# V loaded four keys a partition and put in order by 0/1 products, with experts and slot inputs turned round, in an attention and soft-MoE kernel

## The chip, the cores and the metric

One core of one Trainium2 chip runs the whole kernel. The metric is the time of one execution in device microseconds; the time before is the median of three runs. The profile is one further execution, taken by the hardware profiler, with its own time.

## The reference

Attention over 16 beacon keys and 576 causal keys, for 8 batches of 8 heads, and behind it a soft mixture of experts over all 4608 tokens:

```python
B, H, S, Nb, D = (8, 8, 576, 16, 64)
k_all = np.concatenate([beacon_k, k], axis=2)
v_all = np.concatenate([beacon_v, v], axis=2)
scores = scale * np.matmul(q, k_all.transpose(0, 1, 3, 2))
scores = np.where(causal, -1000000000.0, scores)
a = softmax(scores)                      # over the 592 keys
x = (a @ v_all).transpose(0, 2, 1, 3).reshape(B * S, H * D)   # 4608 x 512
logits = x @ phi                         # 32 slots
d = softmax(logits, over tokens); c = softmax(logits, over slots)
slot_input = d.T @ x                     # 32 x 512, 4 slots for each of 8 experts
slot_out[e] = relu(slot_input[e] @ w1[e]) @ w2[e]             # w1 512 x 1024, w2 1024 x 512
out = c @ slot_out
```

(The softmaxes are written out in the reference, with the maximum subtracted.) Inputs and output are float32.

## The kernel before

Attention works through 32 pairs of heads, four pairs to a batch. The 592 keys and queries of a head are cut into five chunks, four of 128 and one of 80. Each engine runs its own queue strictly in the order in which the kernel records it; there is no scheduler. That order is a hand-written list of words for each pair (`order`, `lists`), the same for pairs with the same number modulo four, and `do` turns a word into instructions:

- `S0` to `S3` (`score`, L280): the score products of a pair into one of two PSUM tiles `scs`, one exp on ScalarE into `ex`, and the causal masks on GpSimd (`mask`, L278). S1 and S3 use the one tile, S0 and S2 the other, and `S0` belongs to the next pair. A list ends, for instance, in `S3 c1 T S0`.
- `A0`, `A1` (`attend`): the products of exp and V for the two heads of the *previous* pair, 15 products a head with a column of ones for the sum. Behind A1, VectorE divides into `xb` (L323, L324).
- `T` (`transp`, L266): 36 small transposes that turn q and k of the pair after the next into `qT`, `kT`, through two `tr` tiles in PSUM that VectorE empties (L268).
- `X01`, `X23`, `X4`, `L0`, `L1`, `D`, `SI`: the routing of an earlier batch: x transposed, logits, their exps `dT` transposed (L405), and the slot inputs (`si_piece`, L416).
- `c0`, `c1`, `cl`: V cast to float16 on GpSimd, from the tiles `vr` and `vl` into `vh`. `d0`, `d1` (`dup`, L335) and `M` (`mask_f`, L306) are on VectorE.

All of T, X, L, D and SI draw their PSUM tiles in turn from one pool, `ps_tr`, with two buffers; a new tile waits until the last reader of the tile before the last is done.

V comes with two neighbouring keys in a partition, 512 bytes in one run (`load_r`), so chunk 0 holds the even keys of the first 256 and chunk 1 the odd ones, and the scores pick their keys with a step of two. The diagonal blocks are folded: 64 rows of each of the two halves make one block (`f_`), whose products take `vd`, a copy of V with the halves apart, 130 columns wide. The beacon's V rows overwrite the first 8 partitions of the first tile (`load_bv`), and that request waits on SP for the tile's own load.

All loads of q, k and V are issued from SP, the 37 loads of expert weights from GpSimd at the ends of the pairs by a table (`want`). A q or k tile has five buffers.

Behind the last pair come the last batch's logits and slot inputs, then the experts: `layer1` with the weights stationary and the slot inputs moving (32 products of 32 columns an expert), a ReLU, and `layer2` with the weights moving, 512 columns in four column groups. `idle_work` is products whose result nobody reads. At last each token's output is one product and one scaling.

The pool of the two tiles and the lists:

```python
ps_tr = ctx.enter_context(tc.tile_pool(name="ps_tr", bufs=2, space=PSUM))
order = ["d1 S1 A0 L1 M S2 A1 S3 cl T S0 D", "S1 A0 X01 M S2 SI A1 S3 T S0",
         "S1 A0 X23 X4 M S2 A1 S3 c0 T S0", "d0 S1 A0 L0 M S2 A1 S3 c1 T S0"]
```

Of the kernel before, what the change touches and what calls it, by code (L numbers as in the profile page):

```python
# [8 lines left out]
FP = mybir.dt.float32  # L9
# [8 lines left out]
def kernel(  # L18
# [12 lines left out]
    nc = tc.nc  # L31
# [22 lines left out]

    def f_(s):
        return [(64 * r, 64, 2 * P * r + s, 2, 2 * P * r, P, P * s) for r in range(2)]

    steps = [  # L60
        f_(0) + f_(1) + [(0, P, 2 * P, 2, 3 * P, U - 3 * P, 2 * P)],
        [(0, P, 2 * P + 1, 2, 3 * P, U - 3 * P, 0), (0, UL, 4 * P, 1, 4 * P, UL, 208)],
        [(0, P, 0, 2, P, U - P, 0)],
        [(0, P, 1, 2, P, U - P, 0)],
# [4 lines left out]
    XF, XG1, XT, XG0 = (0, P), (2 * P, 464), 672, (752, 1216)  # L69

    POS = [0, 2, 1, 3, 4]
    prods = [(P, XF[0], P, 0, 0, 2)] + [(P, XG0[s] + P, P, s, 1, 1) for s in range(2)]
    prods += [(P, XF[1], P, 1, 0, 2)]
    prods += [(P, XG0[s], P, s, 2, 1) for s in range(2)]
    prods += [(P, XG0[s] + 2 * P, P, s, 3, 1) for s in range(2)]
    prods += [(P, XG1[s], P, 2 + s, 3, 1) for s in range(2)]  # L80
    prods += [(P, XG0[s] + 3 * P, UL, s, 4, 1) for s in range(2)]
    prods += [(P, XG1[s] + P, UL, 2 + s, 4, 1) for s in range(2)] + [(UL, XT, UL, 4, 4, 1)]
    first, final = {0, 4, 6, 10}, {3, 5, 9, 14}
# [31 lines left out]
    vrows = v.rearrange("b h s d -> (b h s) d")  # L115

    def load_r(b, r):
        t = vrp.tile([P, H, 2 * D], FP, name="vr", tag="vr")
        vr[(b, r)] = t
        o = b * H * S + 2 * P * r - Nb  # L120
        if b == 0 and r == 0:
            nc.sync.dma_start(
                out=t[:, 1:H, :], in_=vrows[S - Nb:S - Nb + (H - 1) * S].rearrange(
                    "(h s) d -> h s d", s=S)[:, 0:2 * P, :].rearrange(
                        "h (p t) d -> p h (t d)", t=2))
            nc.sync.dma_start(
                out=t[Nb // 2:P, 0, :],
                in_=v[0, 0, 0:2 * P - Nb, :].rearrange("(p t) d -> p (t d)", t=2))
        elif r == 0:
            nc.sync.dma_start(out=t[:, :, :], in_=vrows[o:o + H * S].rearrange(  # L130
                "(h s) d -> h s d", s=S)[:, 0:2 * P, :].rearrange("h (p t) d -> p h (t d)", t=2))
        else:
            nc.sync.dma_start(out=t[:, :, :], in_=v[b, :, 2 * P - Nb:4 * P - Nb, :].rearrange(
                "h (p t) d -> p h (t d)", t=2))

    def load_bv(b):
        nc.sync.dma_start(out=vr[(b, 0)][0:Nb // 2],
                          in_=beacon_v[b].rearrange("h (p t) d -> p h (t d)", t=2))
# [14 lines left out]

    def load_w(x):
        if x < NV:
            m, hs = x, (0, 1)
            t = (wh if x < NW else vrp).tile([P, 2048], F16, name="w", tag="w" if x < NW else "vr")
        else:
            m, hs = NV + (x - NV) // 2, ((x - NV) % 2,)
            t = qkp.tile([P, J * P], F16, name="wx", tag=homes[x - NV])  # L160
# [14 lines left out]
    def w1c(e, c, t):  # L175
        lo = 2 * P * (t // 2) + t % 2
        return wv[(4 * e + c // 2, c % 2)][:, lo:lo + 2 * P - 1:2]

# [7 lines left out]
    nc.sync.dma_start(out=bkf, in_=beacon_k.rearrange("b h n d -> (h n) b d"))  # L186
    load_pair(1)
    load_r(0, 0)
    load_pair(2)
    load_bv(0)  # L190
    load_r(0, 1)
    load_vl(0)
    load_pair(3)
    load_pair(4)
# [11 lines left out]
    fmask = const.tile([P, 2 * P], F16, name="fmask")  # L206
    fm = const.tile([P, 2, P], F16, name="fm")
    nc.gpsimd.memset(fm[:, :, :], 65504.0)
    for base, lo in ((P, 64), (0, 0)):
        nc.gpsimd.affine_select(out=fm[:, :, :], in_=fm[:, :, :], compare_op=AL.is_ge,  # L210
                                fill=0.0, base=base, pattern=[[-1, 2], [1, P]],
                                channel_multiplier=-2)
        nc.gpsimd.tensor_copy(out=fmask[lo:lo + 64, :].rearrange("p (s t) -> p s t", s=2),
                              in_=fm[lo:lo + 64, :, :])
# [7 lines left out]
    vd = [const.tile([P, 2, 2, H, DD], F16, name=f"vd{i}") for i in range(2)]  # L222
    for i in range(2):
        nc.vector.memset(vd[i][:, :, :, :, :], 0.0)
# [6 lines left out]
    nc.vector.memset(siacc[:, :, :], 0.0)  # L231
    siT = const.tile([P, NDC, NSL], F16, name="siT")
    hTz = const.tile([P, E, NFC, NSL], F16, name="hTz")
# [47 lines left out]
    def score(n, st):  # L281
# [3 lines left out]
        for (p0, kn, k0, ks, u0, un, col) in steps[st]:  # L285
            for a in range(2):
                nc.tensor.matmul(  # L287
                    sc[p0:p0 + kn, a, col:col + un],
                    kT[n % 3][64 * a:64 * a + 64, k0:k0 + ks * (kn - 1) + 1:ks],
                    qT[n % 3][64 * a:64 * a + 64, u0:u0 + un],  # L290
                    start=True, stop=True)
# [4 lines left out]
        if st == 0:  # L296
            mask(x[:, :, XG1[0]:XG1[0] + P], [[0, 2], [1, P]], P, -2)
        if st == 1:
            mask(x[:, :, XG1[1]:XG1[1] + P], [[0, 2], [1, P]], P - 1, -2)
            mask(x[0:UL, :, XT:XT + UL], [[0, 2], [1, UL]], 0, -1)  # L300
        if st >= 2:
            mask(x[:, :, XG0[st - 2]:XG0[st - 2] + P], [[0, 2], [1, P]], P + 2 - st, -2)

    def mask_f(n):
        x = ex[n][:, :, 0:2 * P]
        nc.vector.tensor_tensor(out=x, in0=x, in1=fmask[:, :].unsqueeze(1).broadcast_to(  # L306
            [P, 2, 2 * P]), op=AL.min)

    def attend(n, a):
        b, g = divmod(n, H // 2)  # L310
        h = 2 * g + a
        for j, (kn, o, m, c, pos, w) in enumerate(prods):
            dst = avs[0:m, a, pos * DD:(pos + w) * DD]
            if w == 2:
                dst, rhs = dst.rearrange("p (r d) -> p r d", r=2), vd[b % 2][:, c, :, h, :]
            else:
                rhs = vh[b % 2][0:kn, c, h, :]
            nc.tensor.matmul(dst, ex[n][0:kn, a, o:o + m], rhs,  # L318
                             start=j in first, stop=j in final)
# [9 lines left out]
    def cast_r(b, r, eng):  # L329
        eng.tensor_copy(  # L330
            out=vh[b % 2][:, 2 * r:2 * r + 2, :, 0:D].rearrange("p s h d -> p h s d"),
            in_=vr.pop((b, r))[:, :, :].rearrange("p h (s d) -> p h s d", s=2))

    def dup(b, r):
        nc.vector.tensor_copy(out=vd[b % 2][64 * r:64 * r + 64, :, r, :, :],  # L335
                              in_=vh[b % 2][0:64, 2 * r:2 * r + 2, :, :])
# [7 lines left out]
    def xt_piece(b, cs):  # L344
# [3 lines left out]
        for ii, i in enumerate(cs):  # L348
            m = P if i < 4 else UL
            for t in range(NDC):  # L350
                nc.tensor.transpose(  # L351
                    tp[:, ii, t, 0:m],
                    xb[b % 2][0:m, POS[i], 2 * t:2 * t + 2, :].rearrange("p h d -> p (h d)"),
                    idh[0:m, 0:m])
# [318 lines left out]
```

## Time and profile before

| what | value |
| --- | --- |
| median of three runs | 214.31 us (213.91 to 215.2) |
| the profiled execution | 212.98 us, span 211.3 us, mean granted TensorE clock 0.962 |
| TensorE, weight loads | 163.6 us busy in 3526 matmuls, 114.8 us |
| VectorE, ScalarE, GpSimd | 137.0, 127.2 and 114.0 us busy |
| exp of the scores, L294 | 107.3 us, 128 of 870 ns |
| masks on GpSimd, L278 | 62.0 us, 160 of 404 ns |
| score products, L287 | 53.1 us, 576 of them |
| attend, L318 | 44.8 us (65 columns and fewer rows), 22.8 us (130 columns) |
| V casts on GpSimd, L330 | 15.8 us, 15 of 1052 ns |
| M on VectorE, L306; doubling, L335 | 14.8 us, 32 of 464 ns; 9.0 us, 16 of 562 ns |
| weights: 27 loads of 512 KB, 10 of 256 KB | 9.5 us and 11.0 us from issue to landing |
| V: 15 loads of 512 KB | 10.7 us from issue to landing |

A line such as "62.74 0.21 PE L351 MATMUL tr<-idh,xb ... x1 [2.11 <-issue]" of a timeline gives the start and the length in microseconds, the engine, the line of the kernel, the operation, output and inputs, how many like it were merged, and, in brackets, how long the engine stood idle before and what ended that. "Issue" means that nothing which the profile records was waited for. A matmul's length contains some 0.17 us until its result stands in PSUM; the next one can start long before. L12 is line 12 of the kernel before.

### The profile page before, as it was taken

How to read it: one execution, taken by the hardware profiler on the slowest of the kernel's cores; microseconds unless marked ns; L12 is line 12 of the kernel's file. 1: busy time of each engine (PE TensorE's matmuls, PEld its weight loads, DVE VectorE, ACT ScalarE, POOL GpSimd, SP SyncE). 2: the span in 40 equal slices, each digit the busy share in tenths (PEclk: the TensorE clock that was granted, in tenths of full speed). 3: DMA queues.
4: the chain of work that ended last, by engine and by line, in shares of the span. 5: the costliest groups of instructions: out<-in, count | busy, mean ns of one | idle time of the engine just before them, and what ended most of it. 6: DMA issues, size and time to landing. Idle time of an engine off the chain costs nothing.

```text
span 211.3 us, 8131 instructions
## 1 busy us (share of the span) xinstructions
PE 163.6 (77%) x3526; PEld 114.8 (54%) x3526; DVE 137.0 (65%) x284; ACT 127.2 (60%) x185; POOL 114.0 (54%) x264
## 2 busy tenths in 40 slices
PE   2475997997859898887989998798899987888000
PEld 2333765865646676665657776565666764333000
DVE  5747595796658787866996887697856300299200
ACT  2171694897649777875986896697593111199100
POOL 5054389497647765865785897798678210000000
PEclk9999997899999999999999999999999999999755
DMA  6989999999999999999999999999999998089996
GB/s 196 283 197 339 334 284 275 270 268 273 306 254 280 301 229 284 320 278 271 292 276 255 305 266 243 269 215 210 211 212 214 207 210 166 0 298 413 413 414 250
DMA packets 44954, 55.89 MB, mean 265 GB/s; under 512 B 9087, under 2 KB 25975, under 8 KB 44919
## 3 DMA queue, kind: packets, MB, share of 16 engines
q1 hardware_dynamic: 36135, 38.60, 57.7%
q0 software_dynamic: 8784, 16.78, 42.9%
q8 instruction: 27, 0.44, 0.8%
q14 instruction: 8, 0.07, 0.1%
HBM read 62.71 MB, written 9.44 MB: 341 GB/s over the span
## 4 chain that ended last, share of the span: by engine, by line
PE 60%; issue 10%; DVE 10%; DMA 5%; POOL 4%; ACT 2%; SPq 1%; DVEq 0%; ACTq 0%; POOLq 0%
PE av L318 19%; PE sc L287 15%; PE tr L266 8%; DMA vr<-in_v_dram 5%; PE tr L595 4%; PE tr L351 3%; DVE osb L637 3%; PE tr L366 3%; DVE xb L324 2%; PE av L606 2%; ACT ex L294 2%; PE tr L416 2%; POOL ex L278 1%; PE sc L454 1%; DVE qT L268 1%
## 5 line engine op out<-in xcount | busy, mean ns | idle before, releaser
L294 ACT ACTIVATE ex<-sc 128x928 f16<-128x928 f32 (+1 forms) x128 | 107.3, 870 | 45.7 <-PE sc L287 42.3
L278 POOL TENSOR_SCALAR_AFFINE_SELECT ex<-ex 128x256 f16<-128x256 f16 (+1 forms) x160 | 62.0, 404 | 47.5 <-ACT ex L294 47.1
L287 PE MATMUL sc<-qT,kT 64*64 64x128 bf16 (+3 forms) x576 | 53.1, 272 | 4.2 <-issue 1.8
L318 PEld LDWEIGHTS <-ex 128*128 128x128 f16 (+2 forms) x960 | 41.4, 107 | 13.8 <-issue 8.4
L318 PE MATMUL av<-vh,ex 128*128 128x65 f16 (+2 forms) x832 | 44.8, 200 | 3.4 <-POOL ex L278 1.7
L287 PEld LDWEIGHTS <-kT 64*64 64x64 bf16 (+2 forms) x576 | 21.2, 105 | 18.6 <-issue 11.5
L324 DVE TENSOR_TENSOR xb<-av,r 128x640 f16<-128x640 f32 x32 | 26.4, 824 | 1.1
L268 DVE COPY qT<-tr 128x576 bf16<-128x576 bf16 x32 | 23.9, 748 | 2.1 <-PE tr L266 2.1
L268 DVE COPY kT<-tr 128x576 bf16<-128x576 bf16 x32 | 23.9, 747 | 0.8 <-PE tr L266 0.8
L318 PE MATMUL av<-vd,ex 128*128 128x130 f16 x128 | 22.8, 229 | 0.5 <-issue 0.5
L266 PE MATMUL tr<-idb,kf 64*64 64x64 bf16 x576 | 16.0, 200 | 6.2 <-DVE bkT L253 3.4
L266 PE MATMUL tr<-idb,qf 64*64 64x64 bf16 x576 | 16.6, 202 | 4.5 <-DMA qf<-in_q_dram 3.7
L169 POOL DMA_DIRECT2D w<-in_moe_w_dram x27 | 19.4, 721 | 0.0
L266 PEld LDWEIGHTS <-qf 64*64 64x64 bf16 x576 | 12.7, 115 | 11.3 <-issue 6.3
L356 DVE COPY xT<-tr 128x1024 f16<-128x1024 f16 x14 | 9.7, 691 | 13.4 <-PE tr L351 13.4
L266 PEld LDWEIGHTS <-kf 64*64 64x64 bf16 x576 | 13.1, 116 | 6.7 <-issue 6.4
L330 POOL CAST vh<-vr 128x1024 f16<-128x1024 f32 x15 | 15.8, 1052 | 0.0
L306 DVE TENSOR_TENSOR ex<-ex,fmask 128x512 f16<-128x512 f16 x32 | 14.8, 464 | 0.4
L634 ACT ACTIVATE osb<-fp,rc 128x512 f32<-128x512 f32 x18 | 11.3, 685 | 4.5 <-PE fp L632 3.8
L351 PE MATMUL tr<-idh,xb 128*128 128x128 f16 (+1 forms) x140 | 10.3, 216 | 4.0 <-issue 4.0
L637 DVE TENSOR_SCALAR osb<-fp,rc 128x512 f32<-128x512 f32 x18 | 12.3, 746 | 0.7 <-PE fp L632 0.7
L632 PE MATMUL fp<-soh,eLh 128*128 128x512 f16 x36 | 10.6, 377 | 2.4 <-ACT osb L634 1.6
(75 smaller groups left out, 148.5 us busy)
## 6 DMA issues: line engine op xcount, KB each, us to landing
w<-in_moe_w_dram POOLq DMA_DIRECT2D x27, 512.0 KB, 9.5
qf<-in_q_dram SPq DMA_DIRECT2D x32, 288.0 KB, 7.4
kf<-in_k_dram SPq DMA_DIRECT2D x32, 288.0 KB, 8.1
out_dram<-osb SPq DMA_DIRECT2D x16, 512.0 KB, 5.5
vr<-in_v_dram SPq DMA_DIRECT2D x15, 512.0 KB, 10.7
wx<-in_moe_w_dram POOLq DMA_DIRECT2D x10, 256.0 KB, 11.0
vl<-in_v_dram SPq DMA_DIRECT2D x8, 160.0 KB, 6.3
out_dram<-osb SPq DMA_DIRECT2D x4, 256.0 KB, 2.9
```

Source lines behind the costliest of these rows:

```text
L169: nc.gpsimd.dma_start(out=t[:, 0:1024 * len(hs)].rearrange("p (c f) -> p c f", f=1024), in_=src)
L266: nc.tensor.transpose(tp[po:po + 64, j, :], hi, idb[po:po + 64, po:po + 64])
L268: nc.vector.tensor_copy(out=dst[:, Nb:Nb + S].rearrange("p (s j) -> p s j", j=J), in_=tp[:, :, :].rearrange("p j s -> p s j"))
L278: nc.gpsimd.affine_select(out=x, in_=x, compare_op=AL.is_ge, fill=0.0, base=base, pattern=pattern, channel_multiplier=cm)
L287: nc.tensor.matmul(sc[p0:p0 + kn, a, col:col + un], kT[n % 3][64 * a:64 * a + 64, k0:k0 + ks * (kn - 1) + 1:ks], qT[n % 3][64 * a:64 * a + ...
L294: nc.scalar.activation(x[:, :, o:o + w], sc[:, :, 0:w], AF.Exp, scale=scale)
L306: nc.vector.tensor_tensor(out=x, in0=x, in1=fmask[:, :].unsqueeze(1).broadcast_to([P, 2, 2 * P]), op=AL.min)
L318: nc.tensor.matmul(dst, ex[n][0:kn, a, o:o + m], rhs, start=j in first, stop=j in final)
L324: nc.vector.tensor_tensor(out=xb[b % 2][:, :, 2 * g:2 * g + 2, :].rearrange("p i a d -> p a i d"), in0=avv[:, :, :, 0:D], in1=r5[:, :, :]. ...
L330: eng.tensor_copy(out=vh[b % 2][:, 2 * r:2 * r + 2, :, 0:D].rearrange("p s h d -> p h s d"), in_=vr.pop((b, r))[:, :, :].rearrange("p h (s ...
L351: nc.tensor.transpose(tp[:, ii, t, 0:m], xb[b % 2][0:m, POS[i], 2 * t:2 * t + 2, :].rearrange("p h d -> p (h d)"), idh[0:m, 0:m])
L637: nc.vector.tensor_scalar(out=osb[:, j - j0, :], in0=fp_[:, :], scalar1=rc[:, i:i + 1], scalar2=None, op0=AL.mult)
```

## The change

V is loaded with four neighbouring keys in a partition (1 KB in one run), half of the heads in each of two tiles. The casts go into `vc`, which has one buffer. Four products with 0/1 matrices on 32 rows each then put the 128 keys of a chunk in order in PSUM (`v_order`, words `V01` and `V23`, two chunks at a time), and VectorE copies them into `vh` (ScalarE one of two in the first two pairs). With the keys in order, every score takes neighbouring keys, the folding, `vd`, `d0`, `d1` and M go, and all products of attend are 65 columns wide. The words change their order; `S0` stands ahead of `T` where a V word is.

```diff
     steps = [
-        f_(0) + f_(1) + [(0, P, 2 * P, 2, 3 * P, U - 3 * P, 2 * P)],
...
+        [(P, 0, 0, P, 0), (P, 2 * P, 2 * P, U - 2 * P, P)],
+        [(P, 3 * P, 3 * P, U - 3 * P, 0), (UL, 4 * P, 4 * P, UL, 208)],
+        [(P, 0, P, U - P, 0)],
+        [(P, P, P, U - P, 0)],
     ]
...
+    prods = [(j, c, 0 if j == 0 else base[c] + P * j) for j in range(NCH) for c in range(j + 1)]
...
         if st == 0:
-            mask(x[:, :, XG1[0]:XG1[0] + P], [[0, 2], [1, P]], P, -2)
+            mask(x[:, :, 0:2 * P].rearrange("p a (i t) -> p a i t", i=2),
+                 [[0, 2], [0, 2], [1, P]], 0, -1)
+        if st == 1 or st == 3:
+            mask(x[:, :, o:o + P], [[0, 2], [1, P]], 0, -1)
...
     def cast_r(b, r, eng):
         eng.tensor_copy(
+            out=vc[:, :, r * HH:(r + 1) * HH, :].rearrange("p s h d -> p h s d"),
+            in_=vr.pop((b, r))[:, :, :].rearrange("p h (s d) -> p h s d", s=4))
+
+    def v_order(b, cs, engs):
+        tp = {c: ps_tr.tile([P, 512], FP, name="tr", tag="tr") for c in cs}
+        for t in range(4):
+            for c in cs:
+                nc.tensor.matmul(tp[c][:, :], vsel[32 * c:32 * c + 32, t, :],
+                                 vc[32 * c:32 * c + 32, t, :, :].rearrange("p h d -> p (h d)"),
+                                 start=t == 0, stop=t == 3)
+        for c, eng in zip(cs, engs):
+            o, i = vh[b % 2][:, c, :, 0:D], tp[c][:, :].rearrange("p (h d) -> p h d", d=D)
...
+                eng.tensor_copy(out=o, in_=i)
...
-    order = ["d1 S1 A0 L1 M S2 A1 S3 cl T S0 D", "S1 A0 X01 M S2 SI A1 S3 T S0",
-             "S1 A0 X23 X4 M S2 A1 S3 c0 T S0", "d0 S1 A0 L0 M S2 A1 S3 c1 T S0"]
+    order = ["S1 A0 L1 cl S2 A1 D S3 V23 S0 T", "S1 A0 X01 S2 SI A1 S3 T S0",
+             "S1 A0 X23 X4 S2 A1 S3 c0 T S0", "S1 A0 L0 c1 S2 A1 S3 V01 S0 T"]
...
+    lists[0] = "BC S1 S2 BT c0 c1 S3 S0 V01".split()
+    lists[1] = "S1 V23 T0 cl S2 A0 S3 A1 S0 T".split()
+    lists[3] = "S1 A0 S2 A1 S3 S0 T".split()
+    lists[4] = "S1 A0 c1 cl S2 A1 V01 S3 S0 V23 T".split()
```

The beacon's V rows are asked for one or more pairs after the tile's load, from a table, and the first requests stand in another order:

```diff
+    asks = {}
+    for vb in range(1, B):
+        for m, m1, what in ((4 * vb - 6, 0, lambda x: load_r(x, 0)),
+                            (4 * vb - 5, 1, lambda x: load_r(x, 1)),
+                            (4 * vb - 4, 1, lambda x: load_bv(x, 0)),
+                            (4 * vb - 3, 2, load_vl),
+                            (4 * vb - 2, 3, lambda x: load_bv(x, 1))):
+            asks.setdefault(m1 if vb == 1 else m, []).append((what, vb))
...
+    load_bk(0, 1)
     load_pair(1)
     load_r(0, 0)
+    load_r(0, 1)
+    load_bk(1, B)
     load_pair(2)
-    load_bv(0)
-    load_r(0, 1)
     load_vl(0)
+    load_bv(0, 0)
```

The slot inputs of batches 0 to 5 are made with x moving (`si_moving`, five products of 512 columns in four column groups instead of 20 of 32), summed in `siq` and turned once at the end (`si_turn`, word SX in the last list). The experts work in two groups of four, with the slot inputs stationary and the weights moving, four experts in four column groups; the hidden values are turned by eight small products a group. The weights of the last four experts are loaded with all of w1 first (`worder`). `hTz` is cleared at pair 29, not at pair 3:

```diff
+            for c in range(NDC):
+                for i in range(EG):
+                    nc.tensor.matmul(
+                        hp[hf][NSL * i:NSL * i + NSL, :], siT[:, c, :],
+                        wv[(4 * (gr * EG + i) + c // 2, c % 2)][:, 512 * hf:512 * hf + 512],
+                        start=(c == 0), stop=(c == NDC - 1))
...
+    hs1 = layer1(1)
+    turn(0, hs0)
+    for e in range(EG):
+        layer2(e, range(NFC))
+    turn(1, hs1)
+    for e in range(EG, E):
+        for t in range(0, NFC, 2):
+            layer2(e, (t, t + 1))
+            if e >= E - 2 and (e, t) != (E - 1, NFC - 2):
+                idle_work(spare, 2)
...
-            if n == 3 and w == "S1":
-                nc.gpsimd.memset(hTz[:, :, :, :], 0.0)
+            if n == NP - 3 and w == "S1":
+                nc.gpsimd.memset(hTz[:, :], 0.0)
```

## The prediction

> **What bounds the kernel now.** I read the busy rows of the page first, then its chain of waits, then the timeline of TensorE, and last the timelines of the other engines in single pairs of heads. The page:
>
> ```profile
> PE   2475997997859898887989998798899987888000
> ...
> DMA  6989999999999999999999999999999998089996
> GB/s 196 283 197 339 334 284 275 270 268 273 306 254 280 301 229 284 320 278 271 292 276 255 305 266 243 269 215 210 211 212 214 207 210 166 0 298 413 413 414 250
> ...
> PE 60%; issue 10%; DVE 10%; DMA 5%; POOL 4%; ACT 2%; SPq 1%; DVEq 0%; ACTq 0%; POOLq 0%
> ```
>
> A slice is 5.3 us. TensorE is at eight or nine tenths from 32 us to 179 us and holds 60% of the chain. The DMA engines are at nine until 180 us too; the plateau at 210 GB/s from 137 us is the weights alone, and their last piece lands at 179.8 us, 3 us before the experts end. So TensorE sets the pace and the DMA is close behind. "Issue" is 10%. TensorE's timeline shows what it is:
>
> ```profile
> 62.74 0.21 PE L351 MATMUL tr<-idh,xb 80*128 80x80 f16 x1 [2.11 <-issue]
> ...
> 69.21 0.38 PE L266 MATMUL tr<-idb,kf 64*64 64x64 bf16 x12 [0.78 <-issue]
> ...
> 80.48 0.43 PE L351 MATMUL tr<-idh,xb 128*128 128x128 f16 x6 [0.69 <-issue]
> ```
>
> Counted over matmuls and weight loads, such gaps stand only at every 256th instruction, and the page's instruction queue moved 27 packets of 16 KB, which is 256 instructions of 64 bytes. The packet starts about 3.8 us after the last such border, takes 1 us, and TensorE goes on 1.4 us later: 6.2 us from border to border, where an undisturbed TensorE needs 5.2 us for 256. Between 40 and 154 us the gaps sum to 12.3 us, or 2.0 us in a batch of four pairs. A batch takes 18.5 us (transposes of L405 at 54.01 and 146.54, five batches), so 16.5 us without them: 3.8 to 4.2 us a pair.
>
> **What the V change puts on TensorE.** In two of four pairs (pair number 4k+3: V01; 4k+4: V23) eight new products of 512 columns stand in TensorE's queue, behind S3 and ahead of S0 and the transposes T. Everything behind them waits when they wait. First pair 4k+3, with the rows of before that show where each engine is:
>
> ```profile
> 119.53 0.41 POOL L278 TENSOR_SCALAR_AFFINE_SELECT ex<-ex 128x256 f16<-128x256 f16 x1 [0.49 <-ACT ex L294]
> 119.88 1.05 POOL L330 CAST vh<-vr 128x1024 f16<-128x1024 f32 x1
> 120.88 0.41 POOL L278 TENSOR_SCALAR_AFFINE_SELECT ex<-ex 128x256 f16<-128x256 f16 x1
> 121.23 0.39 POOL L273 COPY kT<-bkT 128x16 bf16<-128x16 bf16 x1
> 121.57 1.28 POOL L278 TENSOR_SCALAR_AFFINE_SELECT ex<-ex 128x256 f16<-128x256 f16 x3
> ```
>
> ```profile
> 121.89 0.37 PE L287 MATMUL sc<-qT,kT 64*128 64x464 bf16 x2
> 122.19 0.28 PE L266 MATMUL tr<-idb,qf 64*64 64x64 bf16 x6
> ```
>
> ```profile
> 122.25 0.82 DVE L324 TENSOR_TENSOR xb<-av,r 128x640 f16<-128x640 f32 x1
> 122.99 0.74 DVE L268 COPY qT<-tr 128x576 bf16<-128x576 bf16 x1
> ```
>
> 1. *The second cast.* TensorE is free for V01 at 122.19. V01 reads all heads, so it needs c0 and c1, both on POOL. From 119.53 POOL has: S3's mask 0.41, c0 1.0, S0's mask, now 512 wide (256 wide takes 419 ns, 160 wide 344 ns, so some 0.62), a weight request in four of six batches (0.72, on average 0.48), the kT copy 0.25, S1's two masks 0.75, and c1 1.05. That ends at 124.1: TensorE waits 1.9 us (1.4 without a request, 2.1 with one). At its lowest, were c1 ready, nothing.
> 2. *The products.* Two score products of 464 columns in two row groups start together and take 0.30 us in all (the row at 121.89). Four rounds of two 512-column products at 0.216 us and a change of mode of 0.1 are 0.95 us; one after another they are 1.75. I take 0.95, since the score pairs are the nearest.
> 3. *The evacuation.* There are two buffers for `tr`. V01 fills both, so the q transposes wait for VectorE's first copy and the k transposes for its second. The copy of 128x512 float32 isn't in the trace: 592 half-width columns took 0.47, the 512 of soh 0.75; I take 0.70. The last product ends 0.38 us after its start (L606 shows 0.40), and S0 covers 0.3 to 0.45: 0.55 for q and 0.35 for k, 0.9 in all.
>
> With 0.12 us less for two heads (below): +3.6 us. Pair 4k+4 has no cast ahead of V23, but V23's second buffer is that of D, whose copies stand behind the reciprocal (0.22) and xb (0.82) of A1 on VectorE: V23 waits 0.9. Products 0.95, evacuation 0.9; D's own wait of 0.6 for a T buffer (between S0 and S1 in before) goes: +2.0. Pairs 4k+1 and 4k+2 gain 0.12 and lose 0.15, since A0 now needs S3's masked block in its third product, not its sixth: 0. A batch: +5.6 us.
>
> *Back from the gaps.* At 22 us a batch and 730 instructions, 256 take 7.5 us, longer than the 6.2 us a block needs. The gaps go nearly all: −2.0 us a batch (bounds 0 and −2.0). The Trainium skill, Runtime: NRT & Kernel Launch, Instruction fetch mechanics, calls the crossing of a 16 KiB border "mostly hidden"; this trace shows 0.7 to 2.1 us there, so the trace decides. By that rule the gaps would have another cause, would stay, and the sum would be 250.
>
> Net +3.6 us for each of six batches: **+21.6**. Batch 1 has both orderings in pair 4, V23 waiting for V01's two copies as well: c1 wait 2.7, products 1.9, V23's buffers 0.6, evacuation 0.9, less D's wait and heads: **+5.0**.
>
> **The rest.**
> - Attend: 15 products as before, two of 130 columns become 65 wide: 60 to 30 ns each, 0.06 a head, 3.8 us in all, counted above.
> - Scores: S0 has 464 columns in either form (four 64x64 quarters at once, or two halves); six instructions a pair go: 0, at most −0.1 a pair.
> - VectorE loses M (14.8) and the doubling (9.0), gains 30 copies of 0.7: even. POOL loses one mask a pair (0.2); it is in the walk.
> - Slot inputs: 20 products in 0.51 us become five in two rounds of column groups (L606: eight in 0.55): 0.
> - hTz's memset (1.82) made TensorE wait 1.56 at 32.88; at pair 29 it stands before S1's masks with two weight requests: 0.5. **−1.1.**
> - Start: the second V half is asked for ahead of the beacon rows (before: 10.7, behind a wait on SP), but casts, two orderings and copies lie ahead of the first attend: −2 to +3, taken 0.
> - Requests on SP: 33.0 us of SP's waiting for V goes; TensorE waited for a DMA only at the start (3.7), so 0. The new constants on POOL (some 7 us) end before the first exp's mask near 12.
> - Experts: before 167.65 to 182.86, 1.75 of it gaps. After: layer 1, 64 products in fours at 0.55 for eight, 3.7 with a change of group; two turns with their copy 1.5; layer 2 of experts 0 to 5 2.7; of 6 and 7, seven times two products and two idle ones (0.22 + 0.43 + 0.22) and a last pair, 6.4: 14.3. **−0.9.** The weights from pair 25 on need 40 us back to back; asked for 20 us later they land near 198, ahead of their use near 206, so the idle products are pure cost.
>
> Sum: 21.6 + 5.0 − 1.1 − 0.9 = 24.6 over the profiled run's 212.98 (span 211.3): **238 us**. The median of the three runs is 1.3 above that run, inside what I claim.
>
> **Rivals.**
> - *Casts and D come in time* (POOL and VectorE ahead of TensorE): items 1 and D fall out, 6 x 2.8 = 17 us: 221. For it: POOL is busy 54%. Against: the five POOL rows are back to back.
> - *The weights set the end.* If V's waits fall into time that TensorE loses anyway, the last landing decides. V's 16,384 packets of 512 bytes (27 ns, the median of the packet records; 2304 bytes take 99) become 8,192 of 1 KB (about 48 by a line between): 3.3 us less of 16 engines. The last piece lands at 176.5, one round of products after it, so the end moves from 182.9 to 177.5: 207.6. It decides only if TensorE's loop grows by less than about 3 us, where I sum 26 at the end of the loop. For it: the DMA row. The Trainium skill, DMA: Bandwidth & Descriptors, Specifications, has full rate from 512 bytes on; by that the wider packets give nothing and this rival is at 210.5, but the packet records speak for a gain.
> - *Products one after another*: 14 x 0.8 = 11 more: 249. Against: the score pairs.
> - *The gaps stay* whatever the pace: 12.3 more: 250.
>
> **Numbers.** One per cent is about what a measurement can tell from none. Chances: 238 (230 to 245) 0.60; 221 0.16; about 213, the waits mostly covered, 0.04; 207.6 0.11; 249 and 250 together 0.09. Range 215 to 248: it leaves out the faster case, the even one and part of the last, 0.20. Faster 0.11, same 0.04, slower 0.85.
>
> **What would show it.** TensorE waiting at the ordering products for POOL's cast, some 1.9 us in six pairs; q and k transposes waiting for VectorE's copies of `vh`; fewer and shorter issue gaps in the loop; the last weight landing well ahead of the last expert. Batches near 18.5 us, or a layer 2 that waits for weights, would prove the walk wrong.

## The result

| | before | after |
| --- | --- | --- |
| median of four runs each | 214.75 us (213.91 to 216.0) | 258.69 us (256.44 to 260.68) |
| ratio, 95% interval | | 1.2055 (1.1981 to 1.2128) |
| profiled execution | 212.98 us, span 211.3 | 258.0 us, span 256.3 |
| mean granted TensorE clock | 0.962 | 0.867 |

A fifth slower. Medians are of all runs, ratios and intervals of the undisturbed ones alone, so that the two can differ (most in experiments 10 to 12), and the traces of experiments 1, 3, 11 and 12 are of disturbed runs. The page of the changed kernel, with the lines that answer to those of before (a slice is 6.4 us now), and the granted clock between them:

```profile
PE   2358978988898989689968988976999997988400
...
PEclk9999995795789779977998999998559979999955
DMA  6998869789389889596695798889978999009996
...
PE 48%; POOL 16%; DVE 14%; issue 6%; ACT 5%; DMA 4%; SPq 1%; DVEq 0%; ACTq 0%; POOLq 0%
```

The DMA is no longer at nine throughout, "issue" falls from 10% to 6% of the chain, and GpSimd and VectorE take 30% of it where they had 14%. The row that the prediction did not use has changed most: the clock dips to five and seven tenths again and again.

TensorE's timeline over one V01 and the V23 behind it (start, length, engine, line, operation, and in brackets how long it stood idle and what ended that):

```profile
131.41 1.04 PE L327 MATMUL tr<-vc,vsel 32*128 32x512 f16 x8 [1.75 <-POOL vc L319]
...
133.21 0.47 PE L265 MATMUL tr<-idb,qf 64*64 64x64 bf16 x18 [0.46 <-DVE vh L335]
133.81 0.69 PE L265 MATMUL tr<-idb,kf 64*64 64x64 bf16 x18
...
134.79 1.06 PE L307 MATMUL av<-vh,ex 128*128 128x65 f16 x15
...
139.23 1.03 PE L327 MATMUL tr<-vc,vsel 32*128 32x512 f16 x7 [0.53 <-DVE dT L408]
...
140.84 0.47 PE L265 MATMUL tr<-idb,qf 64*64 64x64 bf16 x18 [0.27 <-DVE vh L335]
```

GpSimd ahead of that V01, with the weight request and the second cast that the prediction had put there:

```profile
128.83 0.71 POOL L150 DMA_DIRECT2D w<-in_moe_w_dram  x1
...
130.33 1.03 POOL L319 CAST vc<-vr 128x1024 f16<-128x1024 f32 x1
```

Each wait that the prediction named is there: V01 behind the second cast on GpSimd, V23 behind D's copies, the transposes behind VectorE's copies of `vh`. What it did not name is in the third and fourth line of TensorE's timeline: the same 18 transposes take 0.47 us at 133.21 and 0.69 at 133.81, and attend 1.06 us where an undisturbed head takes 0.67. From 133.62 to 137.03 TensorE runs at half its clock. Busy time and granted clock of single batches, from pair 4k+3 to the next (the bounds in us, their length, then the busy time and, in brackets, the instructions of TensorE's products, its weight loads, VectorE, ScalarE and GpSimd, then the clock, the DMA's share and GB/s):

```profile
54.20:79.19 24.99, 22.08 (x368) 14.20 (x369) 14.75 (x28) 14.44 (x21) 11.98 (x27) 0.80 0.80 199
79.19:102.82 23.63, 21.08 (x368) 13.81 (x369) 14.75 (x28) 14.45 (x21) 11.29 (x26) 0.86 0.91 229
...
126.97:149.99 23.02, 19.65 (x369) 12.71 (x369) 14.78 (x28) 14.38 (x21) 11.93 (x27) 0.93 0.82 213
149.99:170.96 20.97, 18.32 (x369) 11.95 (x369) 14.68 (x28) 14.33 (x21) 12.65 (x26) 1.00 0.88 213
170.96:199.24 28.28, 23.75 (x344) 14.49 (x344) 14.81 (x28) 14.91 (x23) 17.72 (x35) 0.76 0.94 169
```

The same instructions (368 products) take 20.97 us at the full clock and 24.99 at 0.80: the lower the clock, the longer the batch. (Of the difference, 0.7 us is the weight request that the longer batch has ahead of its second cast.) The prediction's batch is 22.0.

Where the 45.0 us between the two spans lie, by the starts of the pairs (a pair starts with its S1 products), beside the terms of the prediction put on the same stretches:

| stretch | forecast | measured | in experiment 2 |
| --- | --- | --- | --- |
| start to pair 2 | 0 | +4.2 | +4.4 |
| pairs 2 to 6 (batch 1; 5.0 less hTz's wait of 1.56) | +3.4 | +5.0 | +4.3 |
| pairs 7 to 26, five batches | +18.0 | +23.9 | +17.0 |
| pairs 27 to 30 (3.6 and 0.5 for hTz) | +4.1 | +9.4 | +5.7 |
| behind pair 30, experts and output | -0.9 | +2.4 | +1.2 |
| sum | +24.6 | +45.0 | +32.7 |

### The profile page after: what moved, and what is told of

Its sections match the earlier page's. It is cut to its first block, busy times and chain, and to the rows that moved or that the text cites. A ratio compares the mean times of both kernels' runs of the same rounds, so it can differ in the third digit from the quotient of the medians.

```text
span 256.3 us, 7498 instructions
## 1 busy us (share of the span) xinstructions
PE 201.2 (78%) x3212; PEld 122.6 (48%) x3212; DVE 138.3 (54%) x269; ACT 129.5 (51%) x181; POOL 110.2 (43%) x246
## 4 chain that ended last, share of the span: by engine, by line
PE 48%; POOL 16%; DVE 14%; issue 6%; ACT 5%; DMA 4%; SPq 1%; DVEq 0%; ACTq 0%; POOLq 0%
PE av L307 10%; PE tr L327 8%; PE tr L265 8%; PE sc L286 7%; POOL ex L277 6%; DVE vh L335 5%; POOL vc L319 5%; ACT ex L292 4%; POOL w L150 3%; DVE osb L683 3%; DVE xb L313 3%; DMA vr<-in_v_dram 3%; PE tr L365 2%; PE sc L466 2%; PE av L646 2%
## 5 line engine op out<-in xcount | busy, mean ns | idle before, releaser
L277 POOL TENSOR_SCALAR_AFFINE_SELECT ex<-ex 128x256 f16<-128x256 f16 (+2 forms) x128 | 55.4, 445 | 92.0 <-ACT ex L292 91.7
L307 PE MATMUL av<-vh,ex 128*128 128x65 f16 (+2 forms) x960 | 50.8, 209 | 1.7 <-POOL ex L277 1.5
L286 PE MATMUL sc<-qT,kT 64*128 64x464 bf16 (+4 forms) x384 | 49.6, 317 | 1.8 <-DVE kT L272 0.9
L327 PE MATMUL tr<-vc,vsel 32*128 32x512 f16 x128 | 24.7, 467 | 15.7 <-POOL vc L319 10.8
L335 DVE CAST vh<-tr 128x512 f16<-128x512 f32 x30 | 19.5, 689 | 25.3 <-PE tr L327 25.3
L286 PEld LDWEIGHTS <-kT 64*128 64x128 bf16 (+1 forms) x384 | 15.6, 102 | 22.9 <-issue 17.9
L312 DVE RECIPROCAL r<-av 128x10 f32<-128x10 f32 x32 | 7.1, 220 | 31.3 <-PE av L307 30.5
L327 PEld LDWEIGHTS <-vsel 32*128 32x128 f16 x128 | 7.3, 103 | 27.0 <-issue 17.8
L150 POOL DMA_DIRECT2D w<-in_moe_w_dram x27 | 19.4, 721 | 0.0
L680 ACT ACTIVATE osb<-fp,rc 128x512 f32<-128x512 f32 x18 | 11.3, 684 | 13.1 <-PE fp L678 12.4
L319 POOL CAST vc<-vr 128x1024 f16<-128x1024 f32 x15 | 15.5, 1033 | 4.0 <-DMA vr<-in_beacon_v_dram 4.0
L265 PEld LDWEIGHTS <-kf 64*64 64x64 bf16 x576 | 15.8, 124 | 2.7 <-issue 2.1
L683 DVE TENSOR_SCALAR osb<-fp,rc 128x512 f32<-128x512 f32 x18 | 12.3, 746 | 0.7 <-PE fp L678 0.7
```

What stands on the lines that cost most here:

```text
L150: nc.gpsimd.dma_start(out=t[:, 0:1024 * len(hs)].rearrange("p (c f) -> p c f", f=1024), in_=src)
L265: nc.tensor.transpose(tp[po:po + 64, j, :], hi, idb[po:po + 64, po:po + 64])
L277: nc.gpsimd.affine_select(out=x, in_=x, compare_op=AL.is_ge, fill=0.0, base=base, pattern=pattern, channel_multiplier=cm)
L286: nc.tensor.matmul(sc[0:kn, a, col:col + un], kT[n % 3][64 * a:64 * a + 64, k0:k0 + kn], qT[n % 3][64 * a:64 * a + 64, u0:u0 + un], start= ...
L307: nc.tensor.matmul(avs[0:m, a, j * DD:(j + 1) * DD], ex[n][0:kn, a, o:o + m], vh[b % 2][0:kn, c, h, :], start=c == 0, stop=c == j)
L319: eng.tensor_copy(out=vc[:, :, r * HH:(r + 1) * HH, :].rearrange("p s h d -> p h s d"), in_=vr.pop((b, r))[:, :, :].rearrange("p h (s d) - ...
```

## The experiments

**1. The second cast on VectorE.** GpSimd keeps c0, so V01 no longer waits for two casts in a row there.

```diff
-                cast_r(vb, int(w[1]), nc.vector if n < 2 and w == "c1" else nc.gpsimd)
+                cast_r(vb, int(w[1]), nc.vector if w == "c1" else nc.gpsimd)
```

> The second V cast (c1) moves from GpSimd to VectorE in every batch; nothing else changes. Theory A (the waits of TensorE at V01 are GpSimd's cast, and the half clock that follows them costs as much again): the wait of 1.1 to 1.8 us at V01 goes in six batches (about 10 us) and with it most of the half-clock stretches (54.6 us at half clock in the changed kernel): 228 to 238 us, mean clock above 0.92. Theory B (the waits alone; the clock changes nothing that TensorE needs): about 10 us less, 247 to 249 us. If the cast is not what V01 waits for: 258.

Two runs: 232.7 and 238.9 us. One pair 4k+3 with part of the next in its timeline, and two batches:

```profile
117.71 1.03 PE L327 MATMUL tr<-vc,vsel 32*128 32x512 f16 x8
...
119.52 0.47 PE L265 MATMUL tr<-idb,qf 64*64 64x64 bf16 x18 [0.48 <-DVE vh L335]
120.12 0.47 PE L265 MATMUL tr<-idb,kf 64*64 64x64 bf16 x18
...
124.21 1.03 PE L327 MATMUL tr<-vc,vsel 32*128 32x512 f16 x7 [0.53 <-DVE dT L408]
```

```profile
52.13:73.42 21.29, 19.66 (x368) 12.69 (x369) 15.56 (x29) 14.33 (x21) 11.41 (x26) 0.92 0.96 239
...
95.39:115.08 19.69, 18.06 (x370) 11.77 (x368) 14.82 (x28) 14.25 (x21) 10.09 (x25) 1.00 0.93 245
```

The wait ahead of V01 is gone. In the six pairs from 7 on it was 1.1 or 1.8 us, 9.5 us in all, yet the profiled span falls by 19, and the other run is 6 us shorter still: most of the half clock goes with the wait, as theory A had it. Inside the loop it stays only in stretches of 3.4 us behind V23's wait.

**2. The waits stay, filled with work.** From pair 7 on TensorE is given idle products ahead of the ordering, eight before V01 and four before V23, whose result nobody reads. Nothing is taken away.

```diff
         tp = {c: ps_tr.tile([P, 512], FP, name="tr", tag="tr") for c in cs}
+        if fill:
+            idle_work(tp[cs[0]], fill)
...
-                        (nc.vector, nc.scalar if n < 2 else nc.vector))
+                        (nc.vector, nc.scalar if n < 2 else nc.vector),
+                        fill=0 if n < 7 else 8 if w == "V01" else 4)
```

> All waits stay; in the time in which TensorE waits for the cast or for a PSUM buffer, it works on products that nobody reads (eight of 512 columns ahead of V01, four ahead of V23, from pair 7 on). No work is taken away. Theory A (half clock after idle windows is the part that the prediction lacked): the clock stays at 1.0 in the loop, mean above 0.94, and the time falls by 12 to 20 us, to 238 to 246. Theory B (the clock is a by-product, the waits are all): 258 or more, since work is only added.

246.3 us (two runs), ratio 1.155 (1.134 to 1.177).

```profile
122.22 1.90 PE L468 MATMUL tr<-w,idh 128*128 128x512 f16 x8
124.06 1.03 PE L329 MATMUL tr<-vc,vsel 32*128 32x512 f16 x8
...
125.88 0.47 PE L265 MATMUL tr<-idb,qf 64*64 64x64 bf16 x18 [0.48 <-DVE vh L337]
```

```profile
53.65:75.64 21.99, 20.68 (x381) 12.75 (x381) 14.68 (x28) 14.36 (x21) 11.97 (x27) 1.00 0.87 226
75.64:97.62 21.98, 20.67 (x381) 12.75 (x381) 14.67 (x28) 14.35 (x21) 11.24 (x26) 1.00 0.93 229
...
163.56:188.18 24.62, 21.14 (x356) 12.74 (x356) 14.74 (x28) 14.82 (x23) 17.75 (x35) 1.00 1.08 193
```

With 12 more products in a batch and nothing taken away, the kernel is 12.4 us faster. The clock is at 1.00 from 47.8 us to 232, inside the output stage. So the clock costs time of its own, and it is a term that the prediction lacked. Five batches take 21.98 us each, the prediction's 22.0, but that is no proof of its waits: the eight idle products take 1.84 us (122.22 to 124.06) in every batch, as long as the longer waits for the cast and 0.7 longer than the shorter ones.

**3. Without the ordering step.** The products and copies of V01 and V23 are left out and `vh` holds ones, so the output lacks V; all else of the change is there.

```diff
-                v_order(vb, (0, 1) if w == "V01" else (2, 3),
-                        (nc.vector, nc.scalar if n < 2 else nc.vector))
+                pass
```

> The ordering products and their copies are left out, so V is not in the output (ones stand in its place); all loads, casts and the rest of the change stay. Theory A and B: everything that the change costs in the loop hangs on the ordering step (products, its waits and the clock behind them), so the loop falls back to about 18 us a batch with the gaps every 256 instructions back: 210 to 218 us in all, of which some 4 us are the later start. Rival (requests, the order of S0 and T, the masks or the experts cost too): above 222.

207.4 and 211.0 us. Pair 2 begins at 23.27 us (after: 28.27; before: 24.02), and the five batches to pair 27 take 90.2 us where before takes 92.9. The ordering step with all that it brings costs some 49 us, more than the whole loss; the rest of the change is worth some 4 us, as far as two runs can tell.

**4. The start: the beacon keys later.** `BC` and `BT` behind pair 1, since TensorE waited 4.5 us for them at 13.8.

```diff
-    lists[0] = "BC S1 S2 BT c0 c1 S3 S0 V01".split()
-    lists[1] = "S1 V23 T0 cl S2 A0 S3 A1 S0 T".split()
+    lists[0] = "S1 S2 c0 c1 S3 S0 V01".split()
+    lists[1] = "S1 V23 T0 cl S2 A0 S3 A1 S0 T BC BT".split()
```

> The cast and transposes of the beacon keys of batches 1 to 7 (words BC, BT) move from pair 0 to the end of pair 1. In the changed kernel TensorE waits 5.0 us for them at 13.8 us, in front of everything else, and the first attend starts some 4 us later than before. If that wait sets the start: 3 to 4.5 us less, 254 to 255.5. If the first V order sets it (its beacon rows land late): within 1 us of 258.

260.0 us (two runs), 1.3 more than after and within their scatter (ratio 1.1875 to 1.2521): no gain, and neither of the two expected times. V01 begins at 18.29 instead of 17.40, after 7.2 us of waiting for the second cast, and `BT` adds its own wait of 2.5 behind pair 1.

**5. The ordering step moved.** Every product and copy stays; both casts go into pair 4k+2, V01 and V23 between S2 and A1, and D into the next pair. With them the second request for the beacon's V rows comes one pair earlier (not shown).

```diff
-    order = ["S1 A0 L1 cl S2 A1 D S3 V23 S0 T", "S1 A0 X01 S2 SI A1 S3 T S0",
-             "S1 A0 X23 X4 S2 A1 S3 c0 T S0", "S1 A0 L0 c1 S2 A1 S3 V01 S0 T"]
+    order = ["S1 A0 L1 cl S2 V23 A1 S3 S0 T", "S1 A0 D X01 S2 SI A1 S3 T S0",
+             "S1 A0 c0 X23 X4 S2 A1 S3 c1 T S0", "S1 A0 L0 S2 V01 A1 S3 S0 T"]
```

> The changed kernel with every product and copy of the ordering step kept, but placed where their inputs are ready and where nothing waits for their buffers: both casts in pair 4k+2 (POOL), V01 in pair 4k+3 and V23 in pair 4k+4 between S2 and A1, D one pair later. Theory A (the step costs by its waits, 1.9 for the cast, 0.9 for D's copies, 0.9 behind each pair of copies, and by the half clock that follows these waits; the products themselves are 0.95 us twice a batch): kind 3 and kind 0 4.9 us each, kind 1 4.3, kind 2 3.9, a batch 18.0 instead of 23.35, no half clock from pair 7 on, and 218 to 230 us in all, with the start unchanged. Theory B (the eight products of 32 rows, or the copies on VectorE, are too much work in themselves): a batch stays at 21 us or more and the time at 240 or above.

233.3 us (231.0 to 234.5, four runs), ratio 1.091 (1.082 to 1.099).

```profile
92.42 1.37 PE L327 MATMUL tr<-vc,vsel 32*128 32x512 f16 x8
93.72 0.67 PE L307 MATMUL av<-vh,ex 128*128 128x65 f16 x15
...
94.82 0.47 PE L265 MATMUL tr<-idb,qf 64*64 64x64 bf16 x18
95.13 0.45 PE L265 MATMUL tr<-idb,kf 64*64 64x64 bf16 x18
```

```profile
71.36:90.69 19.33, 18.48 (x369) 12.03 (x369) 14.37 (x28) 14.03 (x21) 11.44 (x27) 1.00 1.04 262
...
148.48:173.40 24.92, 21.30 (x344) 13.37 (x344) 14.52 (x28) 14.71 (x23) 17.76 (x35) 0.86 1.07 191
```

No wait for the cast, none of the transposes for the copies, a batch of 19.3 us at the full clock. Theory B falls: the same products and copies cost 0.7 us a batch over before's 18.6 where they wait for nothing, and 4.8 where they stand in the changed kernel. (Before's 18.6 contains the 2.0 us of gaps, which are gone in both.) I had expected 18.0; V01 and V23 take 1.30 us to the next product instead of 0.97, and D costs 0.8 in its new place. 27 of the 45 us between the spans come back.

**6. The start: V's rows without those that the beacon's replace,** so that the beacon's requests need not wait on SP for the halves.

```diff
+        if b == 0:
+            for lo, hi in ((Nb // 4, 64), (64, P)):
+                nc.sync.dma_start(out=t[lo:hi, :, :], in_=v[0, r * HH:(r + 1) * HH, 4 * lo - Nb:4 * hi - Nb, :]...
...
     load_r(0, 0)
+    load_bv(0, 0)
     load_r(0, 1)
+    load_bv(0, 1)
```

> The changed kernel with the first batch's V rows requested without the rows that the beacon's replace, so that the beacon's requests need not wait on SP until the halves have landed, and each beacon request right behind its half. Theory A (the first order waits for the second cast, and that for beacon rows that are requested late): pair 2 begins 2 to 4 us earlier than in the changed kernel (24 to 26 instead of 28.3) and the time falls by as much, to 254 to 257. Theory B (the bytes of q, k and both V halves set the start, whatever the order of requests): pair 2 begins within 1 us of 28.3 and the time is within 1 us.

256.7 us (254.5 to 261.2, four runs), ratio 1.194 (1.185 to 1.203), which overlaps that of after. Pair 2 begins at 29.11. GpSimd has its rows at 11.4 instead of 14.4, but the second cast stands on VectorE behind `BC`, whose keys are there at 14.45. Alone this gains nothing either.

**7. The experts alone,** in the kernel of before: weights moving, hidden units turned by 0/1 products, the new order of the weights.

> The kernel of before with the experts alone in the new form (weights moving, hidden units turned by 0/1 products, the new order of the weights and the idle products between the last). Theory A (the prediction's walk of this stage): 0.9 us faster than before, 212 to 215. Theory B (the two waits for the ReLUs and for the turned units, seen after the change, eat it): within 0.5 us of before or up to 1 slower. Theory C (the 5 us by which the kernel without the ordering step lies under the one before come from this stage): 208 to 211.

213.77 us (ten runs) against 213.97 (13 runs), ratio 0.9995 (0.9945 to 1.0045): no difference.

```profile
169.39 1.05 PE L613 MATMUL sc<-w,siT 128*32 128x512 f16 x16 [0.75 <-ACT hs L618]
...
173.23 1.91 PE L640 MATMUL av<-w,hTz 128*32 128x512 f16 x32 [0.77 <-DVE hTz L632]
...
175.81 0.83 PE L640 MATMUL av<-w,hTz 128*32 128x512 f16 x12 [0.39 <-DVE hTz L632]
```

The stage runs from 167.59 to the first output product at 183.94, 0.3 us longer than before's 167.65 to 183.72. The forecast of 0.9 less had the copies behind the turns in, but not the wait for ScalarE's ReLU. Both this 0.9 and no gain at all lie inside the interval; the trace speaks for none.

**8. Both ends.** Start as in 4 and 6 together; the weights' requests spread (`0.78 * n`, then 19, 20, 22, 24) instead of four after pair 25.

> The changed kernel with its two ends alone repaired. Start: V's rows of the first batch requested without those that the beacon's replace, and the beacon keys' cast and transposes of batches 1 to 7 moved behind pair 1; each alone changed the start by 4 us the wrong way or not at all. End: the weights' requests spread, one or two after each pair instead of four after pair 25. Theory A (the first order waits for two things, the second cast behind the beacon keys' cast on VectorE and the beacon's value rows, and either alone hides the other): pair 2 begins at 23.5 to 25 instead of 28.3; and the four requests stand ahead of masks: the last batch, pairs 27 to 30, takes 25 to 27 us instead of 28.3; together 250 to 254. Theory B (the products and copies of the first order themselves set the start): pair 2 begins at 27 or later.

255.2 us (253.8 to 256.6, four runs), ratio 1.183 (1.174 to 1.193). Half of the expectation held. The last batch takes 25.5 us instead of 28.3, as expected. Pair 2 begins at 29.19, not at 24. The start in TensorE's timeline:

```profile
15.18 1.89 PE L327 MATMUL tr<-vc,vsel 32*128 32x512 f16 x8 [3.11 <-DVE vc L319]
...
17.82 1.89 PE L327 MATMUL tr<-vc,vsel 32*128 32x512 f16 x8 [0.40 <-DVE vh L335]
...
20.47 0.69 PE L265 MATMUL tr<-idb,qf 64*64 64x64 bf16 x18 [0.76 <-DVE vh L335]
...
28.19 0.93 PE L249 MATMUL tr<-idb,bk 128*128 128x128 bf16 x7 [2.56 <-DVE bk L244]
```

V01 does begin 2.2 us earlier than after, but `BT` takes its wait of 2.56 in front of pair 2, and from V01 to the first transposes it is 5.3 us as in the changed kernel (17.40 to 22.68). That stretch, not the wait ahead of it, is what the start gained: experiment 3, which lacks it, begins pair 2 5.0 us earlier. Eight products take 1.89 us where they take 1.03 later. These are half-clock lengths (18 transposes 0.69), although the page's clock row shows nine there: the first clock record stands at 24.4 us before and at 27.8 us after, and the row takes the time ahead of it as full.

**9. All repairs of 5 and 8,** V01 and V23 right behind A0, and V's rows as in 6 for all batches.

> All repairs together: both ends as in the other run of this call, both casts in pair 4k+2, V01 and V23 right behind A0, the logits' products behind A1, D a pair later. Theory A (the waits and the half clock were the cost; the products and their copies are 2 us a batch): batches of 18.5 to 19.3 us, pair 4 at 5 to 7, the last batch at 22 to 23: 217 to 224. Theory B (what remains over the kernel of before is as large as in the run with moved products alone): 229 or above. Neither theory has it under the kernel of before, 214: two products' time and copies a batch more than before, and nothing of size that before has and this has not.

236.2 us (234.8 to 239.0, four runs), ratio 1.093 (1.085 to 1.101): no faster than 5 alone. Four batches take 18.8 to 19.4 us, but in the other one a pair lasts 13.1:

```profile
80.21 1.89 PE L327 MATMUL tr<-vc,vsel 32*128 32x512 f16 x8 [5.55 <-POOL vc L319]
```

GpSimd's cast there had waited 5.1 us for beacon rows that SP asked for at 64 us and that were there, by the profile, at 79. Theory A's batches held, its sum did not: a new wait, for V's rows, comes in. Why these rows took 15 us was not tried.

**10. Work in the waits of the start.** Idle products of 128 columns in the changed kernel: 16 ahead of the first transposes, 14 and 32 ahead of the two beacon transposes, 14 ahead of V01.

```diff
+    def warm(m):
+        for _ in range(m):
+            nc.tensor.matmul(avs[:, 0, 384:512], idb[:, :], idb[:, :], start=True, stop=True)
```

> The changed kernel with idle products of 128 columns on TensorE (nobody reads them) in the waits of its start: 16 before the first transposes, 14 before the first beacon transposes, 32 before those of batches 1 to 7, 14 before the first V01. Theory A (TensorE runs at half its clock up to 27.8 us, where the first clock record stands: 18 transposes take 0.69 instead of 0.47, the eight products 1.89 instead of 0.95, so the two orderings that the start gains cost 5 us instead of 3): with work in the waits the full clock comes before the first V01, V01 takes 1.0 to 1.3, pair 2 begins at 24.5 to 26.5 instead of 28.3, and the time is 254 to 257. Theory B (the start's products are long for another reason, such as cold operands): V01 stays at 1.9 and pair 2 within 0.7 of 28.3.

251.6 to 257.7 us, median 256.6 of four runs, without an interval.

```profile
7.53 0.47 PE L265 MATMUL tr<-idb,qf 64*64 64x64 bf16 x18
...
8.94 1.96 PE L531 MATMUL av<-idb 128*128 128x128 bf16 x32
14.21 0.56 PE L249 MATMUL tr<-idb,bk 128*128 128x128 bf16 x7 [3.31 <-DVE bk L244]
...
17.23 1.89 PE L327 MATMUL tr<-vc,vsel 32*128 32x512 f16 x8 [0.67 <-DVE vc L319]
```

The first half worked: the transposes of pair 1 take 0.47 instead of 0.69, at 7.5 us, and the first record of full clock stands at 5.4. But at the full clock the 32 products are through in 2 us, 3.3 us of waiting are left, the clock halves at 15.6, and V01 is at 1.89 again. Pair 2 begins 0.9 us earlier. That work decides the clock in the start is shown; that a fast V01 would bring the start back to forecast stays open.

**11. The same in the kernel of before,** with hTz's memset at pair 29 as in the change: 16, 14 and 26 idle products.

> The kernel of before with the one small part of the change that the prediction priced as a gain, hTz's memset at pair 29 instead of pair 3 (-1.1), and idle products in the waits of its start (16 at the beginning, 14 before the first beacon transposes, 26 before the k transposes that wait at 18.3). Theory A (half clock until 24.4 us and again from 34.7 to 38.1, after the memset's wait, costs 2 to 3 us in all): 211 to 213.5 against 214 to 215, faster by 0.5 to 1.5%. Theory B (weights and DMA set the end whatever TensorE does at the start): no difference, within 0.4%.

Medians 212.86 us (209.4 to 221.4, six runs) and 213.11; the ratio, from three of the six runs, is 0.988 (0.980 to 0.996). The profiled run (213.5) has the full clock from 9.9 to 44.1 us, begins pair 2 at 22.11 instead of 24.02 and pair 5 at 32.51 instead of 36.80. By pair 31 all is given back, 158.46 against 156.67. Its timeline has longer gaps of the kind that the prediction described, and behind four of them, though not behind that at 62.66, 3.41 us of half clock each (from 44.07, 81.61, 102.09 and 139.64). The traced run of before has none behind its gaps. The clock row of this run and two of the gaps:

```profile
PEclk9999999969999997999699999969999999999955
...
43.26 0.46 PE L318 MATMUL av<-vh,ex 128*128 128x65 f16 x8 [1.40 <-issue]
...
62.66 0.20 PE L318 MATMUL av<-vh,ex 128*128 128x65 f16 x1 [1.97 <-issue]
```

The gain at the start is real in the trace, and the half clock behind the gaps eats into it; how much of the loss is the clock and how much the gaps was not separated. Whether the kernel is faster, the scattered runs don't settle; it is the only complete version here that may beat both.

**12. What is left.** Experiment 5 with the spread requests of 8 and the idle products of 10.

> The changed kernel with the ordering step moved (as in the run of that name, 233.3 us) and the two repairs that are left: idle products in the waits of the start, and the weights' requests spread instead of four after pair 25. Theory A (the start's half clock, 2 to 3 us, and the burst's wait of 2.5 us with 6.8 us of half clock behind it): pair 2 at 24.5 to 26, the last batch at 20 to 22 instead of 24.9, 225 to 229 us. Theory B (the slack turns into waits for V's rows, as in the run with all repairs): a stall of several us before an ordering step, 231 or above.

229.7 us (227.0 to 231.1, four runs), ratio 1.069 (1.060 to 1.079).

```profile
112.47:131.80 19.33, 18.47 (x368) 12.03 (x369) 14.36 (x28) 14.02 (x21) 11.92 (x27) 1.00 1.03 269
...
151.14:171.74 20.60, 18.94 (x344) 12.01 (x344) 14.44 (x28) 14.48 (x23) 15.79 (x30) 1.00 0.88 153
```

The time lies between the two expectations. The last batch falls from 24.9 to 20.6 us, as expected; pair 2 still begins at 28.26, and pairs 2 to 6 run at a clock of 0.80. There is no stall as in 9.

## Why the prediction was wrong

It forecast 238 us (215 to 248): the direction was right, the size 20.7 us too small, outside the range. The failed step is the sum of "What the V change puts on TensorE": each wait stands there at its own length, and all work behind it at full speed. The runs showed a second price, half of TensorE's clock behind the waits. A second term failed beside it, the start, taken at 0 and measured at +4.2. The clock's term is 12.3 us between the spans of the changed kernel and of experiment 2: 6.9 in the five batches, 3.7 in the last, 0.7 in pairs 2 to 6 and 1.2 at the end, less 0.2 at the start. Of these, only the five batches and the last have idle products in their waits; in the other parts the two traces differ in their clock without them.

A hint stood on the page of before. Its clock row, which the prediction did not quote, has one dip ahead of the output stage, right behind the one long wait that the prediction did price, 1.56 us for hTz's memset at 32.88; the transposes at 35.16 take 0.69:

```profile
PEclk9999997899999999999999999999999999999755
...
32.88 0.20 PE L318 MATMUL av<-vh,ex 128*128 128x65 f16 x1 [1.56 <-POOL ex L278]
...
35.16 0.69 PE L266 MATMUL tr<-idb,qf 64*64 64x64 bf16 x18
```

The hint gives the price, not how often it is paid: the longer gap ahead of 62.74 (2.11 us) in the same trace is not followed by half a clock.

By its own steps:

- *The second cast*, 2.1 us with a weight request, 1.4 without, 1.9 on average: measured 1.8 with one (58.6, 107.3, 131.4, 176.8) and 1.1 without (82.9, 153.7). The step is right, each wait 0.3 us shorter than forecast.
- *The products*, 0.95 by the score pairs: 0.97 from V01's first product to S0's at 131.41. The rival of one after another fell.
- *The evacuation*, 0.55 and 0.35: with the full clock of experiment 1, 0.48 for q and 0.29 for k behind V01, 0.27 and 0.29 behind V23: 0.77 and 0.56 in all, where the sum had 0.9 twice. The copy takes 0.69, by the prediction 0.70. D's copies: 0.92 between V23's first two products, by the prediction 0.9.
- *The gaps go*: right. Where the full clock holds, batches are the same to 0.02 us (21.97 to 21.99 in experiment 2), with no gap left. The rival of gaps that stay, 250, was nearer to the measured time by chance; its mechanism is not in the trace.
- *The batch*, +3.6: +3.4 in experiment 2 (109.9 us for five against 92.9), +4.8 as it was. That 3.4 is so near is in part luck, since the idle products outlast the shorter waits. The changed kernel's one batch at the full clock, 20.97, without a request ahead of its second cast, is 2.4 over before's mean. With 0.7 for a request in three of the five batches, an estimate from these rows, work and waits are +2.8 a batch, and the clock's part in the five is 9.7 us, not 6.9. Batch 1 had 5.0 less 1.6: measured 5.0, at a clock of 0.80.
- *Start, taken 0 with -2 to +3*: +4.2. The prediction names the casts, two orderings and copies ahead of the first attend, but puts no price on them. From V01 to the transposes they take 5.3 us, at half clock.
- *The last batch*: beside the clock, four weight requests stand on GpSimd ahead of pair 26's masks and, in pair 27, A0's third product waits 1.6 us for the mask. The rows of before had the price of a request (0.72); the prediction counted one in the pairs 4k+3 and two at pair 29, not the four after pair 25. Spread in experiment 8, the batch is 2.8 us shorter, the clock's part included.
- *Experts, -0.9*: no difference in experiment 7, +0.3 in its trace.
- *Casts in time*, 221, and *the weights set the end*, 207.6: fell. The last weight landed at 218.0, well ahead of layer 2's end at 227.5, as forecast in kind (198 ahead of 206). Two slips of its arithmetic move nothing here: by the prediction's own steps the second rival without the gain of wider packets is at 210.9 (207.6 and 3.3), not 210.5, and 256 instructions at 22 us for 730 take 7.7 us, not 7.5.

The excess of 20.4 us over the forecast is thus 12.3 by the clock as far as experiment 2 held it, 4.4 at the start, 0.9 in pairs 2 to 6 (where it had no fill), 1.6 in the last batch with its requests, and 2.1 behind the loop, less 1.0 by which the five batches were dearer in the forecast. Of the 2.1, 1.2 is the experts' share by the trace of experiment 7; the other 0.9 was not looked into. By the estimate above, the clock's share is some 15 us, and the five batches were 3.8 us dearer in the forecast.

## What to carry to other kernels

A wait on TensorE costs its length and then, if it is followed by half a clock, nearly as much again: here 12 us, beside some 15 us of waits ahead of V01 and V23 from pair 7 on. So read the granted clock of before for dips and ask which wait stands ahead of each. An instruction moved in front of a queue is cheap where its inputs are ready and nobody needs its buffer; the same step cost 4.8 us a batch at the end of a pair and 0.7 in its middle, each after the 2.0 us of gaps that went. And a wait that can't be removed may be worth filling with work that nobody reads.

## What the hardware showed

The half clock does not need an idle stretch. The two stretches around 133.62 in the changed kernel, and one of the same length later that was not followed by half clock:

```profile
130.21:133.62 3.41, 1.75 (x30) 0.91 (x30) 1.42 (x3) 1.22 (x2) 1.50 (x3) 1.00 1.07 309
133.62:137.03 3.41, 3.29 (x48) 2.14 (x42) 1.62 (x3) 1.01 (x3) 2.04 (x5) 0.50 1.05 324
150.69:154.10 3.41, 2.38 (x36) 1.48 (x34) 1.36 (x3) 2.92 (x6) 3.32 (x7) 1.00 1.06 236
```

The stretches of one clock are multiples of 3.41 us (3.41, 6.83, 10.24, 13.65) but for the last of each trace, which ends with it, and the clock is 0.5 or 1 in all records. The Trainium skill, TensorE: Matmul & The Clock Gate, Part 1: The HAM clock gate, has these two values and a window of 3413 ns, which these records bear out. Its table lets the clock fall after at least one idle window; here a window in which TensorE was busy for 1.75 of 3.41 us, with no wait over 1.75, was enough. One with 2.38 busy was not, but one with 2.82 (113.14 to 116.55) was, and so was one with 3.13 (205.30 to 208.71), behind the loop. So no bound by busy time alone separates the cases, half a clock can also come without a long wait ahead of it, and what exactly is counted stays open.

The same section gives the cold ramp less than 1% of a typical span. Here the start, with one wait for DMA after another, stays at half clock until 24.4 us before and 27.8 after: 18 transposes take 0.69 us against 0.47. Experiment 11, with idle products in those waits, reaches the full clock at 9.9 us and begins pair 5 4.3 us earlier, 2% of the span.
